# A chunked delta rule with two MoE layers: triangular inverses by 16-row blocks, joined by TensorE

## The chip, the cores and the metric

One core of a Trainium2 chip runs the whole kernel. The metric is device time in microseconds (us), the median of several runs; lower is better. TensorE (PE) multiplies matrices, VectorE (DVE), ScalarE (ACT) and GpSimd (POOL) work elementwise, and SyncE (SP) issues every DMA of this kernel. Each engine takes its own instructions strictly in the order in which they were emitted.

## The reference

```python
def _attn_ref(q, k, v, beta):                 # batch 4, 8 heads, 768 steps, head dim 48
    k_n = k / (norm(k) + 1e-06)
    for t in range(S):
        y[:, :, t] = einsum('bhd,bhde->bhe', q[:, :, t], state)
        v_old = einsum('bhde,bhd->bhe', state, k_n[:, :, t])
        state = state + beta_t * einsum('bhd,bhe->bhde', k_n[:, :, t], v_t - v_old)

x = y, heads side by side                     # (3072, 384)
h = maximum(x @ w_in, 0); x = (h * h) @ w_out                      # d_ff 2048
out = (sigmoid(x @ w_gate) * (x @ w_val)) @ w_out                  # d_ff 1536
```

All of it is float32. The weights arrive as 64-bit floats, and the kernel turns them into pairs of 32-bit parts.

## The kernel before, in words

The sequence is cut into 12 chunks of 64 steps. Two chunks (st 0 and 1) make a **pass** g, so there are 6 passes. In a pass the delta rule is solved for all 32 heads of the batch at once: the products of keys (`am`, token `a`) give a unit triangular 64-by-64 matrix per head and chunk, its inverse is built in `t64`, and with it the chunk's update (`t`), its output (`y`) and the next state (`s`) are matrix products. The pass's output `x` (512 tokens) then goes through the first MoE layer in 16 blocks of 128 hidden features: `h,n` (n is 16 g + block), the squared ReLU on ACT, `g,n` (the low part, on DVE) and `o,n`. The second MoE layer follows after the last pass.

The inverse has two levels. The two 32-by-32 diagonal blocks of each matrix are inverted by substitution on DVE: `ti` transposes `am` into `xi` and clears `tt`, `r,g,i` does three rows j of the substitution (tokens `r,g,0` to `r,g,10`, rows 31 to 1; each row is a multiply at L385 and a subtract at L392, and rows below 22 take two of each), `to` transposes the result back into `t64` and `t1` makes the transposed copy `t1`. TensorE then makes the block beside them from two products, `n` (L414) and `w` (L429), with ACT evicting each.

During passes 0 and 1 the weights of the first MoE layer are also converted, one block f of 16 at a time: `f` loads 768 KB, `hi` (ACT), `b` and `b2` (DVE, two instructions each), `lo` (POOL), `ch` (ACT), `cl` (POOL) and `sl` (a DMA that stores the low part in DRAM). `li,n` and `lw,n` fetch such low parts back; `h,n` and `o,n` cannot run before their block f = n is converted.

The order of everything up to the last blocks of pass 5 is a list written out by hand, `ORDER`. Its tokens are run one after another, and each token emits its instructions on whatever engines it uses. So the list fixes the order within every engine's queue, SP's too, and nothing reorders it afterwards. `xlo`, the low part of `x`, has two buffers in turn.

Of the kernel before, what the change touches and what calls it, by code (L numbers as in the profile page):

```python
# [31 lines left out]
z,0,0 s,0,0 hi,3 f,4 b,2 b2,2 a,1,1 ks,0,1 lo,2 ch,2 cl,2 sl,2 a,1,0 ti,1 x,0,0 ti,1,1 li,1 b,3 t,0,1 hi,4 y,0,1
ti,1,3 b2,3 li,0 s,0,1 z,0,1 x,0,1 f,5 lo,3 ch,3 cl,3 sl,3 r,1,0 r,1,1 f,6 lw,0 v,1,0 kc,1,1 kc,1,0 k2,1,0 q,1,1
hi,5 b,4 h,0 li,2 b2,4 lw,1 g,0 h,1 li,3 lo,4 f,7 b,5 ch,4 cl,4 r,1,2 b2,5 sl,4 q,1,0 lw,2 r,1,3 hi,6 g,1 h,2
li,4 lo,5 f,8 b,6 ch,5 cl,5 r,1,4 b2,6 hi,7 b,7 sl,5 kt,2,1 o,0 lo,6 f,9 ch,6 lw,3 cl,6 sl,6 g,2 h,3 li,5 b2,7
kn,2,0 o,1 r,1,5 r,1,6 hi,8 lw,4 kn,2,1 g,3 h,4 li,6 r,1,7 lo,7 f,10 ch,7 cl,7 hi,9 kt,2,0 sl,7 sq,2,1 r,1,8 o,2
b,8 sq,2,0 lw,5 sv,1,0 b2,8 lo,8 f,11 ch,8 cl,8 r,1,9 hi,10 g,4 h,5 li,7 sl,8 sm,2,0 p,1,0 b,9 r,1,10 b2,9 lo,9
ch,9 cl,9 o,3 lw,6 sl,9 g,5 h,6 li,8 to,1 b,10 hi,11 b2,10 o,4 v,1,1 p,1,1 lw,7 t1,1 lo,10 f,12 ch,10 cl,10 g,6
h,7 li,9 sv,1,1 n,1,0 b,11 b2,11 sl,10 lo,11 f,13 hi,12 ch,11 cl,11 sm,2,1 o,5 n,1,1 ks,1,0 lw,8 sl,11 g,7 h,8
li,10 w,1,0 b,12 b2,12 hi,13 no,2 b,13 o,6 w,1,1 lo,12 ch,12 b2,13 lw,9 cl,12 t,1,0 lo,13 f,14 ch,13 sl,12 cl,13  # L40
a,2,0 g,8 h,9 li,11 sl,13 a,2,1 o,7 lw,10 hi,14 ti,2 g,9 h,10 li,12 y,1,0 ti,2,1 b,14 ti,2,3 z,1,0 b2,14 o,8
s,1,0 lw,11 r,2,0 lo,14 f,15 ch,14 cl,14 sl,14 g,10 h,11 li,13 r,2,1 k2,1,1 hi,15 o,9 lw,12 ks,1,1 x,1,0 b,15
b2,15 r,2,2 g,11 h,12 li,14 t,1,1 y,1,1 z,1,1 lo,15 ch,15 cl,15 r,2,3 o,10 lw,13 sl,15 r,2,4 g,12 h,13 li,15
o,11 lw,14 r,2,5 g,13 h,14 li,16 r,2,6 o,12 lw,15 x,1,1 r,2,7 g,14 h,15 li,17 r,2,8 o,13 kc,2,0 lw,16 w2,0,0
g,15 h,16 li,18 s,1,1 r,2,9 q,2,0 o,14 kn,3,0 lw,17 r,2,10 w2,0,1 g,16 h,17 li,19 kn,3,1 o,15 kc,2,1 v,2,0 lw,18
sq,3,0 w2,0,2 po,0 k2,2,0 sq,3,1 g,17 h,18 li,20 w2,0,3 to,2 o,16 lw,19 kt,3,1 sm,3,0 kt,3,0 w2,0,4 t1,2 p,2,0
g,18 h,19 li,21 sm,3,1 w2,0,5 sv,2,0 n,2,0 w2,1,0 o,17 lw,20 no,3 g,19 h,20 li,22 q,2,1 w2,1,1 o,18 lw,21 ks,2,0
g,20 h,21 li,23 n,2,1 w,2,0 w2,1,2 o,19 w2,1,3 lw,22 a,3,0 g,21 h,22 li,24 w2,1,4 a,3,1 v,2,1 o,20 w,2,1 lw,23
w2,1,5 ti,3 t,2,0 w2,2,0 g,22 h,23 li,25 k2,2,1 sv,2,1 y,2,0 o,21 z,2,0 lw,24 ti,3,1 ti,3,3 w2,2,1 g,23 h,24
li,26 s,2,0 r,3,0 o,22 lw,25 w2,2,2 p,2,1 r,3,1 g,24 h,25 li,27 ks,2,1 w2,2,3 o,23 lw,26 r,3,2 w2,2,4 g,25 h,26  # L50
li,28 w2,2,5 t,2,1 r,3,3 o,24 x,2,0 w2,3,0 lw,27 g,26 h,27 li,29 y,2,1 r,3,4 o,25 lw,28 w2,3,1 g,27 h,28 li,30
# [28 lines left out]
"""  # L80

@with_exitstack
def kernel(
# [18 lines left out]
    nc = tc.nc  # L102
# [3 lines left out]
    work = ctx.enter_context(tc.tile_pool(name="work", bufs=2))  # L106
# [61 lines left out]
    at = ExitStack()  # L168
# [44 lines left out]
    for i in range(NF2 * 3 // 2):  # L213
        cs = slice(i * 2 * DM, (i + 1) * 2 * DM)
# [15 lines left out]
    def att_ps():  # L230
        return ps_a.tile([128, 512], F32, tag="att", name="att")
# [135 lines left out]
    def turn_in(g, q=None):  # L370
# [203 lines left out]
    po = [None] * KD  # L574
# [35 lines left out]
    def keep_warm(n):  # L610
# [232 lines left out]
```

## Time and profile before

| | |
|---|---|
| median of 3 runs | 1154.88 us (1154.48 to 1156.91) |
| the profiled execution | 1156.59 us, its span 1154.9 us |
| PE busy | 1034.7 us, 90% of the span |
| DVE busy | 613.3 us, 53% |
| ACT, POOL busy | 426.6 us, 143.8 us |
| mean granted clock of TensorE | 0.971 of full speed |

The shares are means over a start in which PE is often idle and a long rest in which it is nearly always busy. What a change in the start is worth has to be read from the start alone.

### The profile page before, as it was taken

The numbers are of one execution on the slowest core, as the hardware profiler recorded it, in microseconds if no ns is written. First come the engines' busy times: TensorE is split into PE (matmuls) and PEld (weight loads), VectorE is DVE, ScalarE is ACT, GpSimd is POOL, SyncE is SP. The second block draws the span as 40 slices with busy tenths as digits, with TensorE's granted clock in tenths as the row PEclk, the third lists the DMA queues.
The fourth block names the chain that finished last, engine by engine and source line by source line (L and its number), as shares of the span: only waits on it lengthen the run. The fifth ranks groups of instructions, "written<-read, shape, count | busy, mean of one in ns | idle before, by whom it ended". The sixth has DMA issues, their size and how long they took to land.

```text
span 1154.9 us, 24743 instructions
## 1 busy us (share of the span) xinstructions
PE 1034.7 (90%) x10608; PEld 874.2 (76%) x10608; DVE 613.3 (53%) x1250; ACT 426.6 (37%) x680; POOL 143.8 (12%) x106
## 2 busy tenths in 40 slices
PE   2184757899999999899999999999999999999997
PEld 2173545677787787688888888888888888888886
DVE  5968999986797689389443244322222222222222
ACT  2043435445456355344745564321222222222211
POOL 2122435302002001101110010100100001001000
PEclk9997787899999999899999999999999999999999
DMA  9325933577469447746744554101010010100101
GB/s 254 91 84 145 293 106 128 168 206 208 132 186 283 153 150 225 181 137 192 210 126 160 185 171 137 42 15 41 1 56 1 1 55 1 55 1 1 28 1 28
DMA packets 85214, 133.84 MB, mean 116 GB/s; under 512 B 33648, under 2 KB 66032, under 8 KB 85104
## 3 DMA queue, kind: packets, MB, share of 16 engines
q1 hardware_dynamic: 85104, 132.26, 38.8%
q8 instruction: 83, 1.36, 0.5%
q14 instruction: 27, 0.22, 0.1%
HBM read 104.69 MB, written 22.81 MB: 110 GB/s over the span
## 4 chain that ended last, share of the span: by engine, by line
PE 78%; DVE 11%; DMA 4%; SPq 2%; issue 2%; ACT 2%; POOL 1%; DVEq 0%; ACTq 0%; POOLq 0%
PE gv L716 26%; PE o L586 14%; PE h L549 14%; PE o L746 13%; DVE tt L392 3%; DVE tmp L385 2%; PE att L343 2%; PE att L472 1%; PE att L494 1%; DMA il<-w1d 1%; DVE wt L141 1%; DMA w1d<-wl 1%; DMA kc<-in_kq_dram 1%; PE att L460 1%; PE att L496 1%
## 5 line engine op out<-in xcount | busy, mean ns | idle before, releaser
L724 DVE TENSOR_TENSOR p<-sg,gv 128x512 f32<-128x512 f32 x72 | 49.5, 687 | 284.1 <-PE gv L716 284.1
L716 PE MATMUL gv<-xhi,w2l 128*128 128x512 f32 x432 | 123.3, 394 | 0.0
L716 PE MATMUL gv<-xhi,w2h 128*128 128x512 f32 x432 | 123.3, 394 | 0.0
L716 PE MATMUL gv<-xlo,w2h 128*128 128x512 f32 x432 | 123.2, 393 | 0.0
L562 ACT ACTIVATE gg<-h 128x512 f32<-128x512 f32 x96 | 57.2, 596 | 169.5 <-PE h L549 148.4
L586 PE MATMUL o<-gh,il 128*128 128x512 f32 x288 | 114.8, 399 | 0.0
L722 ACT ACTIVATE sg<-gv 128x512 f32<-128x512 f32 x72 | 43.0, 598 | 182.2 <-PE gv L716 182.2
L726 ACT CAST ph<-p 128x512 fp32r<-128x512 f32 x72 | 44.7, 620 | 159.0 <-DVE p L724 159.0
L586 PE MATMUL o<-gl,w1h 128*128 128x512 f32 x216 | 87.0, 403 | 13.0 <-DVE gl L571 13.0
L549 PE MATMUL h<-xhi,il 128*128 128x512 f32 x288 | 84.9, 404 | 14.1 <-DMA il<-w1d 14.1
L746 PE MATMUL o<-w2h,pl 128*128 128x384 f32 x288 | 97.4, 338 | 0.0
L746 PE MATMUL o<-w2h,ph 128*128 128x384 f32 x288 | 97.2, 338 | 0.0
L746 PE MATMUL o<-w2l,ph 128*128 128x384 f32 x288 | 97.1, 337 | 0.0
L716 PEld LDWEIGHTS gv<-xlo,w2h 128*128 128x128 f32 x432 | 81.3, 188 | 18.9
L716 PEld LDWEIGHTS gv<-xhi,w2l 128*128 128x128 f32 x432 | 81.1, 188 | 18.8
L571 DVE TENSOR_TENSOR gl<-gg,gh 128x512 fp32r<-128x512 f32 x96 | 71.7, 748 | 42.8 <-ACT gg L565 42.7
L392 DVE TENSOR_TENSOR tt<-tt,tmp 128x21 f32<-128x21 f32 (+37 forms) x312 | 90.2, 322 | 2.1
L586 PE MATMUL o<-gh,w1h 128*128 128x512 f32 x216 | 90.3, 418 | 0.0
L716 PEld LDWEIGHTS gv<-xhi,w2h 128*128 128x128 f32 x432 | 80.3, 188 | 12.8
L385 DVE TENSOR_TENSOR tmp<-xi,tt 128x21 f32<-128x21 f32 (+37 forms) x312 | 83.4, 300 | 1.3
L549 PEld LDWEIGHTS h<-xhi,il 128*128 128x128 f32 x288 | 55.8, 195 | 27.9 <-DMA il<-w1d 15.7
L728 DVE TENSOR_TENSOR pl<-p,ph 128x512 fp32r<-128x512 f32 x72 | 49.9, 692 | 49.4 <-ACT ph L726 49.4
(111 smaller groups left out, 1768.5 us busy)
## 6 DMA issues: line engine op xcount, KB each, us to landing
il<-w1d SPq DMA_DIRECT2D x192, 192.0 KB, 3.6
raw<-in_w_dram SPq DMA_DIRECT2D x25, 768.0 KB, 6.0
w1s<-in_w_dram SPq DMA_DIRECT2D x9, 768.0 KB, 6.0
w2d<-y SPq DMA_DIRECT2D x18, 384.0 KB, 3.9
t<-w2d SPq DMA_DIRECT2D x12, 576.0 KB, 3.8
w1d<-wl SPq DMA_DIRECT2D x16, 384.0 KB, 2.8
kn<-in_kn_dram SPq DMA_DIRECT2D x12, 384.0 KB, 4.8
v<-in_vn_dram SPq DMA_DIRECT2D x12, 384.0 KB, 5.2
```

Of the source, the lines that this page charges most:

```text
L385: nc.vector.tensor_tensor(out=tv[i], in0=xi[:, 0:j, j].unsqueeze(2).to_broadcast([128, j, n]), in1=tt[:, j, lo:hi].unsqueeze(1).to_broadca ...
L392: nc.vector.tensor_tensor(out=tt[:, 0:j, lo:hi], in0=tt[:, 0:j, lo:hi], in1=tv[i], op=ALU.subtract)
L549: nc.tensor.matmul(out=ps[:, cs], lhsT=w[:, kc * 128:kc * 128 + 128], rhs=x[:, kc, cs], start=(i == 0 and kc == 0), stop=(i == 2 and kc == ...
L562: nc.scalar.activation(out=gg, in_=ps, func=ACTF.Relu)
L571: nc.vector.tensor_tensor(out=gl, in0=gg, in1=gh.bitcast(F32), op=ALU.subtract)
L586: nc.tensor.matmul(out=po[m], lhsT=w[:, cs], rhs=x, start=(f == 0 and i == 0), stop=(f == NF1 - 1 and i == 2),)
L716: nc.tensor.matmul(out=ps, lhsT=w[:, kc * 128:kc * 128 + 128], rhs=x[:, kc, :], start=(i == 0 and kc == 0), stop=(i == 2 and kc == KD - 1),)
L722: nc.scalar.activation(out=sg, in_=pss[0], func=ACTF.Sigmoid)
L724: nc.vector.tensor_tensor(out=p, in0=sg, in1=pss[1], op=ALU.mult)
L726: nc.scalar.copy(out=ph, in_=p)
L728: nc.vector.tensor_tensor(out=pl, in0=p, in1=ph.bitcast(F32), op=ALU.subtract)
L746: nc.tensor.matmul(out=po2[m], lhsT=x[:, cs], rhs=w, start=(f == 0 and i == 0), stop=(f == NF2 - 1 and i == 2),)
```

## The change

In passes 0 and 1 the substitution covers only the 16-by-16 diagonal blocks: 15 rows instead of 31, both blocks of a 32-by-32 block in one instruction (`row16`). The 32-by-32 inverse is then joined from its parts by TensorE: `ja` (a product of `am` and `t64` on top of minus the identity, which a 128-column matmul with `ib` and `cb` puts there first), `jb` (a product with `t1`) and `jc` (the same for the transposed copy), with evictions on ACT. `cj` makes the constants on POOL, in a tile that takes a buffer of `xlo` before its use. Passes 2 to 5 keep the 32-row substitution. The rest of the change is a new `ORDER` list.

```diff
+BLOCK = (16, 16, 32, 32, 32, 32)
 ORDER = """
-kn,0,1 v,0,0 kt,0,0 sq,0,1 sm,0,1 q,0,0 kn,0,0 sq,0,0 v,0,1 f,1 be kt,0,1 kc,0,0 sm,0,0 no,0 cs hi,1 f,0 kn,1,0
+v,0,0 kn,0,1 kn,0,0 kt,0,0 sq,0,1 be kt,0,1 sm,0,1 sq,0,0 f,1 kc,0,0 q,0,0 v,0,1 sm,0,0 no,0 hi,1 f,0 cs q,0,1
...
+    join_t = work.tile([128, KD * GT], F32, tag="xlo", name="join")
+    nf = join_t[:, 0:1024].rearrange("p (u c) -> p u c", u=32)
+    cb = join_t[:, 1024:1280].bitcast(BF16).rearrange("p (u c) -> p u c", u=32)
+    ib = join_t[:, 1280:1344].bitcast(BF16)
...
+    def join_constants():
+        for t, v in ((ib, 1.0), (cb, -1.0), (nf[:, :, 0:16], 1.0)):
+            nc.gpsimd.memset(t, v)
+        def diagonal(t, pattern, base):
+            nc.gpsimd.affine_select(
+                out=t, in_=t, pattern=pattern, base=base, channel_multiplier=-1, compare_op=ALU.is_equal, fill=0.0
+            )
+        diagonal(ib, [[1, 128]], 0)
+        for q in range(4):
+            diagonal(cb[quad(q)], [[0, 32], [1, 16]], 16)
+            diagonal(nf[quad(q), :, 0:16], [[0, 32], [1, 16]], 0)
+    def both(t, at, *dims):
+        return bass.AP(t.tensor, t.offset + at, [list(t.ap[0]), [16 * 33, 2], *dims])
+    def row16(j):
+        n = 16 - j
+        tv = tmp[1][:, 0:2 * j * n].rearrange("p (b c i) -> p b c i", b=2, i=n)
+        nc.vector.tensor_tensor(
+            out=tv, in0=both(xi, j, [32, j], [0, n]), in1=both(tt, 33 * j, [0, j], [1, n]), op=ALU.mult
+        )
+        t = both(tt, j, [32, j], [1, n])
+        nc.vector.tensor_tensor(out=t, in0=t, in1=tv, op=ALU.subtract)
-    def rows(i):
-        for j in range(31 - 3 * i, max(0, 28 - 3 * i), -1):
-            row(j)
+    def rows(g, i):
+        b = BLOCK[g]
+        for j in range(b - 1 - 3 * i, max(0, b - 4 - 3 * i), -1):
+            (row16 if b == 16 else row)(j)
     def turn_1(g):
         nc.vector.transpose(out=t1.rearrange("p u c -> p c u"), in_=tt)
+        if BLOCK[g] == 32:
+            for q in (0, 2):
+                nc.scalar.copy(out=t64[quad(q), :, 0:32], in_=t64[quad(q), :, 32:64])
+    def join_a(g, i):
+        if i == 0:
+            join_ps[g] = att_ps()
+            nc.tensor.matmul(out=join_ps[g], lhsT=ib, rhs=cb.rearrange("p u c -> p (u c)"), start=True, stop=False)
+        psv = join_ps[g].rearrange("p (u c) -> p u c", u=32)
+        for u in range(16 * i, 16 * i + 16):
+            for q in range(4):
+                c = 32 * (q % 2)
+                nc.tensor.matmul(out=psv[32 * q:32 * q + 16, u, :], lhsT=am[quad(q), u, c:c + 16],
+                                 rhs=t64[quad(q), u, 48:64], start=False, stop=u == 31)
+        if i == 1:
+            nc.scalar.mul(out=nf[:, :, 16:32], in_=psv, mul=-1.0)
+    def join_b(g, i):
...
+                nc.tensor.matmul(out=psv[quad(q), u, :], lhsT=t1[quad(q), u, :], rhs=nf[quad(q), u, 16:32], ...)
+        if i == 1:
+            nc.scalar.copy(out=t64[:, :, 48:64], in_=psv)
+            for q in (0, 2):
+                nc.scalar.copy(out=t64[quad(q), :, 0:32], in_=t64[quad(q), :, 32:64])
+    def join_c(g):
...
+                nc.tensor.matmul(out=psv[quad(q), u, :], lhsT=nf[quad(q), u, :], rhs=t1[quad(q), u, 0:16], ...)
+        for q in (0, 2):
+            nc.scalar.copy(out=t1[quad(q), :, 0:16], in_=psv[quad(q)])
```

What the new list moves is seen in the engines' queues. A matmul counts once here, and the trace has two PE instructions for each float32 one. First SP's queue at the start of the program, before and then changed (`w1s` and `raw` are blocks of weights, `k_114` is the tile `k2`):

```order
L267 DMA kn<-in_kn_dram 128x768
L272 DMA v<-in_vn_dram 128x768
L256 DMA kt<-in_kq_dram 48x1024 x2
L262 DMA q<-in_kq_dram 48x1024 x2
L267 DMA kn<-in_kn_dram 128x768
L272 DMA v<-in_vn_dram 128x768
L126 DMA w1s_137<-in_w_dram 128x1536
L621 DMA beta_t<-in_beta_dram 128x192
L256 DMA kt<-in_kq_dram 48x1024 x2
```

```order
L280 DMA v<-in_vn_dram 128x768
L275 DMA kn<-in_kn_dram 128x768 x2
L264 DMA kt<-in_kq_dram 48x1024 x2
L707 DMA beta_t<-in_beta_dram 128x192
L264 DMA kt<-in_kq_dram 48x1024 x2
L127 DMA w1s_137<-in_w_dram 128x1536
```

The second `kn` load stood behind four loads of other tensors; it is now the third transfer. Next PE's queue in pass 0, between the scores `p` (L343, now L351) and the update `t` (L460, now L546), before and then changed (`t_107` is `t64`, and `xi` holds `t1`):

```order
L343 MATMUL att<-q,kc 64x64 x64
L414 MATMUL att<-t_107,am 32x32 x64
L429 MATMUL att<-n,xi 32x32 x64
L460 MATMUL att<-v,t_107 64x48 x32
L494 MATMUL att<-pm,u_112 64x64 x32
```

```order
L351 MATMUL att<-q,kc 64x64 x64
L451 MATMUL att<-join 128x512
L458 MATMUL att<-t_107,am 16x16 x128
L473 MATMUL att<-join,xi 32x16 x128
L488 MATMUL att<-xi,join 32x16 x64
L500 MATMUL att<-t_107,am 32x32 x64
L515 MATMUL att<-n,xi 32x32 x64
L546 MATMUL att<-v,t_107 64x48 x32
```

The join's 321 matmuls stand ahead of `n` and `w`. Last DVE's queue in pass 1, around the second half of pass 0's `x` (`xlo<-xr`), before and then changed:

```order
L481 TENSOR_TENSOR state<-state,att 128x8x48 x2
L115 TENSOR_TENSOR xlo<-xr,xhi 128x3x256
L385 TENSOR_TENSOR tmp_111<-xi,tt 128x31
L392 TENSOR_TENSOR tt<-tt,tmp_111 128x31
L385 TENSOR_TENSOR tmp_111<-xi,tt 128x60
L392 TENSOR_TENSOR tt<-tt,tmp_111 128x30x2
```

```order
L407 TENSOR_TENSOR tmp_111<-xi,tt 128x110
L411 TENSOR_TENSOR tt<-tt,tmp_111 128x2x11x5
L407 TENSOR_TENSOR tmp_111<-xi,tt 128x120
L411 TENSOR_TENSOR tt<-tt,tmp_111 128x2x10x6
L116 TENSOR_TENSOR xlo<-xr,xhi 128x3x256
L567 TENSOR_TENSOR state<-state,att 128x8x48 x2
L138 TENSOR_SCALAR y<-wt 128x768
```

The first six rows of pass 1's substitution now stand ahead of that `xlo`, and the two state additions behind it.

## Rows read from the trace of the kernel before

**Rows 1.** Busy us by stretch (instructions), engines PE, PEld, DVE, ACT, POOL; then clock, DMA, GB/s.
```profile
0.00:100.00 100.00, 41.75 (x1152) 38.76 (x1152) 70.75 (x169) 26.14 (x39) 21.86 (x27) 0.97 0.49 131
100.00:230.00 130.00, 88.82 (x1297) 70.62 (x1298) 125.08 (x214) 55.16 (x85) 51.89 (x28) 0.80 0.59 181
230.00:260.00 30.00, 28.72 (x179) 23.11 (x178) 26.76 (x104) 13.71 (x22) 2.29 (x1) 0.99 0.70 200
260.00:1155.00 895.00, 875.41 (x7984) 741.71 (x7982) 390.68 (x764) 331.57 (x536) 67.72 (x50) 0.99 0.34 102
```
**Rows 2.** Waits of DVE and PE, 100 to 230: total us, times, longest.
```profile
DVE xlo L115 <- ACT xhi L114: 5.4, 2, 4.5
PE o L586 <- DVE gl L571: 13.0, 3, 8.0
PE h L549 <- DMA il<-w1d: 12.8, 1, 12.8
```
**Rows 3.** Timeline of the start: start us, us, engine, line, operation.
```profile
7.73 1.98 PE L332 MATMUL att<-kt 48*64 48x64 f32 x62 [0.60 <-DMA kt<-in_kq_dram]
10.60 0.84 ACT L289 ACTIVATE kn<-kn 128x768 f32<-128x768 f32 x1 [5.62 <-DMA kn<-in_kn_dram]
22.32 3.81 DVE L376 STREAM_TRANSPOSE xi<-am 32x1024 f32<-32x1024 f32 x2
```
**Rows 4.** Timeline of DVE in pass 0's substitution.
```profile
28.83 0.19 DVE L385 TENSOR_TENSOR tmp<-xi,tt 128x31 f32<-128x31 f32 x1
29.81 0.25 DVE L385 TENSOR_TENSOR tmp<-xi,tt 128x87 f32<-128x87 f32 x1
30.10 0.25 DVE L392 TENSOR_TENSOR tt<-tt,tmp 128x87 f32<-128x87 f32 x1
34.18 1.29 DVE L349 TENSOR_TENSOR pm<-att,mask 128x512 f32<-128x512 f32 x2 [0.38 <-PE att L343]
46.70 0.55 DVE L137 TENSOR_SCALAR y<-wt 128x768 uint32<-128x768 uint32 x1
47.28 0.96 DVE L141 SCALAR_TENSOR_TENSOR wt<-wt,y 128x768 uint32<-128x768 uint32 x1
54.39 0.95 DVE L294 TENSOR_REDUCE s<-kn 128x16 f32<-128x768 f32 x1
57.26 2.18 DVE L401 STREAM_TRANSPOSE t<-tt 128x1024 f32<-128x1024 f32 x1
```
**Rows 5.** Busy us of L385 alone, then L392, in passes 0 and 1.
```profile
28.83:57.25 28.42, 12.10 (x52) 1.00 0.39 93
101.00:163.10 62.10, 19.67 (x52) 0.75 0.73 221
...
28.83:57.25 28.42, 13.54 (x52) 1.00 0.39 93
101.00:163.10 62.10, 18.32 (x52) 0.75 0.73 221
```
**Rows 6.** Timeline of ACT and PE: a pair of small evictions, and small matmuls.
```profile
61.61 1.20 ACT L420 ACTIVATE n<-att 32x512 f32<-32x512 f32 x2
65.02 1.91 PE L429 MATMUL att<-n,xi 32*32 32x32 f32 x62 [0.18 <-ACT n L420]
72.23 3.44 PE L472 MATMUL att<-u,k 64*64 64x48 f32 x60 [0.52 <-ACT yt L499]
183.34 1.20 PE L429 MATMUL att<-n,xi 32*32 32x32 f32 x64
```
**Rows 7.** Timeline of POOL: start-up work, and a weight step beside a DVE multiply.
```profile
1.02 0.53 POOL L357 TENSOR_SCALAR_AFFINE_SELECT mask<-mask 64x64 f32<-64x64 f32 x2
4.63 0.30 POOL L364 MEMSET state<- 128x256 f32 x1
100.91 1.86 POOL L206 TENSOR_TENSOR wl<-wt,w1h 128x768 fp32r<-128x768 f32 x1 [4.31 <-ACT w1h L202]
101.01 1.82 DVE L385 TENSOR_TENSOR tmp<-xi,tt 128x31 f32<-128x31 f32 x1
```

More of the change, by code (lines that the diff above doesn't have):

```diff
@@ L32 @@
[L32 to L51, printed above, removed]
@@ new lines @@
+t1,3 g,33 h,34 li,36 po,1 sv,3,0 p,3,0 w2,5,1 o,32 lw,35 kt,4,1 sm,4,0 kt,4,0 sm,4,1 g,34 h,35 li,37 kc,3,1
+w2,5,2 n,3,0 o,33 ks,3,0 w2,5,3 lw,36 no,4 g,35 h,36 li,38 v,3,1 w2,5,4 n,3,1 w,3,0 o,34 k2,3,0 w2,6,0 lw,37
+w2,5,5 g,36 h,37 li,39 w,3,1 o,35 q,3,1 lw,38 a,4,0 t,3,0 w2,6,1 g,37 h,38 li,40 a,4,1 k2,3,1 o,36 sv,3,1 y,3,0
+w2,6,2 lw,39 ti,4 g,38 h,39 li,41 w2,6,3 s,3,0 z,3,0 ti,4,1 o,37 lw,40 w2,6,4 ti,4,3 p,3,1 g,39 h,40 li,42 r,4,0
+w2,7,0 w2,6,5 o,38 ks,3,1 lw,41 g,40 h,41 li,43 r,4,1 w2,7,1 o,39 lw,42 t,3,1 r,4,2 g,41 h,42 li,44 w2,7,2
@@ new lines @@
+kc,5,1 o,58 lw,61 r,5,5 w2,12,4 g,60 h,61 li,63 w2,13,0 w2,12,5 r,5,6 o,59 q,5,0 lw,62 x,4,1 g,61 h,62 li,64
+r,5,7 w2,13,1 o,60 lw,63 s,4,1 g,62 h,63 li,65 w2,13,2 r,5,8 o,61 w2,13,3 lw,64 r,5,9 g,63 h,64 li,66 p,5,0
+w2,13,4 r,5,10 o,62 lw,65 v,5,0 w2,13,5 g,64 h,65 li,67 to,5 o,63 lw,66 po,3 sv,5,0 t1,5 g,65 h,66 li,68 n,5,0
+ks,5,0 o,64 q,5,1 w2,14,0 lw,67 g,66 h,67 li,69 n,5,1 v,5,1 w,5,0 o,65 k2,5,1 lw,68 t,5,0 w2,14,1 g,67 h,68
+li,70 k2,5,0 w,5,1 o,66 w2,14,2 lw,69 g,68 h,69 li,71 w2,14,3 y,5,0 o,67 sv,5,1 lw,70 w2,14,4 w2,15,0 g,69 h,70
@@ new lines @@
+li,72 s,5,0 w2,14,5 o,68 lw,71 p,5,1 g,70 h,71 li,73 ks,5,1 w2,15,1 o,69 z,5,0 lw,72 w2,15,2 g,71 h,72 li,74
+w2,15,3 o,70 t,5,1 lw,73 w2,15,4 g,72 h,73 li,75 x,5,0 w2,16,0 o,71 w2,15,5 lw,74 y,5,1 g,73 h,74 li,76 z,5,1
+w2,16,1 o,72 lw,75 g,74 h,75 li,77 w2,16,2 o,73 w2,16,3 lw,76 g,75 h,76 li,78 w2,16,4 o,74 w2,17,0 lw,77 w2,16,5
+g,76 h,77 li,79 o,75 lw,78 w2,17,1 g,77 h,78 li,80 o,76 x,5,1 w2,17,2 lw,79 g,78 h,79 li,81 w2,17,3 o,77 lw,80
+w2,17,4 g,79 h,80 li,82 w2,17,5 o,78 lw,81 g,80 h,81 li,83 o,79 lw,82 po,4 g,81
@@ L404, in turn_1 @@
         nc.vector.transpose(out=t1.rearrange("p u c -> p c u"), in_=tt)
+        if BLOCK[g] == 32:
+            for q in (0, 2):
+                nc.scalar.copy(out=t64[quad(q), :, 0:32], in_=t64[quad(q), :, 32:64])
+    join_ps = {}
+    def join_a(g, i):
+        if i == 0:
+            join_ps[g] = att_ps()
+            nc.tensor.matmul(
+                out=join_ps[g], lhsT=ib, rhs=cb.rearrange("p u c -> p (u c)"), start=True, stop=False
+            )
+        psv = join_ps[g].rearrange("p (u c) -> p u c", u=32)
+        for u in range(16 * i, 16 * i + 16):
+            for q in range(4):
+                c = 32 * (q % 2)
+                nc.tensor.matmul(
+                    out=psv[32 * q:32 * q + 16, u, :], lhsT=am[quad(q), u, c:c + 16], rhs=t64[quad(q), u, 48:64],
+                    start=False, stop=u == 31,
+                )
+        if i == 1:
+            nc.scalar.mul(out=nf[:, :, 16:32], in_=psv, mul=-1.0)
+            del join_ps[g]
+    def join_b(g, i):
+        if i == 0:
+            join_ps[g] = att_ps()
+        psv = join_ps[g].rearrange("p (u c) -> p u c", u=32)
+        for u in range(16 * i, 16 * i + 16):
+            for q in range(4):
+                nc.tensor.matmul(
+                    out=psv[quad(q), u, :], lhsT=t1[quad(q), u, :], rhs=nf[quad(q), u, 16:32], start=True, stop=True
+                )
+        if i == 1:
+            nc.scalar.copy(out=t64[:, :, 48:64], in_=psv)
+            for q in (0, 2):
+                nc.scalar.copy(out=t64[quad(q), :, 0:32], in_=t64[quad(q), :, 32:64])
+            del join_ps[g]
+    def join_c(g):
+        ps = att_ps()
+        psv = ps.rearrange("p (u c) -> p u c", u=32)
+        for u in range(32):
+            for q in (0, 2):
+                nc.tensor.matmul(
+                    out=psv[quad(q), u, :], lhsT=nf[quad(q), u, :], rhs=t1[quad(q), u, 0:16], start=True, stop=True
+                )
         for q in (0, 2):
-            nc.scalar.copy(out=t64[quad(q), :, 0:32], in_=t64[quad(q), :, 32:64])
+            nc.scalar.copy(out=t1[quad(q), :, 0:16], in_=psv[quad(q)])
     def n_piece(g, st):
@@ L621 @@
         k2=load_k2, be=lambda: nc.sync.dma_start(out=beta_t, in_=beta), cs=constants, sq=squares, sm=sums, no=norms,
-        a=scores_a, sv=scale_v, p=scores_p, ti=turn_in, r=lambda g, i: rows(i), to=turn_out, t1=turn_1,
+        a=scores_a, sv=scale_v, p=scores_p, ti=turn_in, r=rows, cj=join_constants, ja=join_a, jb=join_b, jc=join_c, to=turn_out, t1=turn_1,
         n=n_piece, w=w_piece, ks=ks_piece, t=t_piece, s=s_piece, y=y_piece, x=x_split, d=keep_warm,
```

67 lines of the change are left out of this document (36 added, 31 removed).

## The prediction

> **What bounds the kernel now.** I read the busy times by stretch first, then the waits, then the timeline of the start. The stretches [rows 1] show three states. To 100 us PE works 42 of 100 us. From 100 to 230 PE works 89 of 130 us while DVE works 125: DVE is the bound. From 230 on PE is: 28.7 of 30 us, then 875 of 895. What is won before 230 therefore reaches the end undiminished, as long as the PE work behind it stays the same, and what is done for DVE after 230 is worth nothing.
>
> In the DVE-bound stage the waits of PE say how DVE paces it [rows 2]: 13.0 us for `gl`, which stands in DVE's queue behind rows of the substitution, and 12.8 us for one low part from DRAM, the end of the conversion of a weight block whose DVE steps stand in the same queue. DVE itself waited only 5.4 us, nearly all of it once, 4.5 us for the first pass's `x`. Ahead of the stage the path is a chain: loads, norms, three transposes, pass 0's substitution, the two products `n` and `w`, the update, `y`, its transfer, `x`.
>
> **The change part by part.**
>
> *Loads and norms.* The second `kn` load was the seventh transfer issued, and its square started at 10.60; transfers three and four, the first `kt` pair, had landed by 7.73 [rows 3]. It is now the third, so I put its square at 7.7. From that square to the end of the last transpose (22.32 + 3.81 = 26.13) the chain took 15.5 us and is the same now: the substitution can start at 23.2. Before it started at 28.83 [rows 4], since a conversion step and a mask multiply stood ahead of it; in the new list those come later. The end of the loads that this rests on could lie 2 us to either side.
>
> *The constants (`cj`).* They are nine selects and three memsets on POOL behind the start-up work that ends at 4.9, ahead of the memset of `tt` that the first row needs. A select of 64 columns takes 0.27 us [rows 7]. Most of the new ones have 512 columns: at least 0.27 us each (2.4 us for nine), at most eight times that (2.2 us, some 18 us for eight and a small one). They end between 8 and 24 us. I take the middle, where they are hidden by the 23.2 above; the upper end costs some 2 us.
>
> *Pass 0's substitution.* Before, it ran from 28.83 to 57.26, 28.4 us. In it lie two conversion steps (0.55 + 0.96 each), a mask pair with its wait (1.7) and a reduction (0.95), 5.7 us together [rows 4]: the 31 rows cost 22.7 us, of which about 1.5 is one held instruction. Now there are 15 rows of two instructions with 30 to 128 elements, 91 on the mean. One of 87 elements is followed by the next after 0.29 us (29.81 to 30.10), so 30 of them cost 8.6 us. The new list puts three conversion steps and two mask pairs between, 7.1 us. The transpose `to` then starts at 23.2 + 8.6 + 7.1 = 38.9 and ends at 41.1; before it ended at 59.4.
>
> *The join in pass 0.* This is the added cost, and it stands on the path: `ja`, an eviction, `jb`, `jc`, and only then `n`, since all are in PE's queue ahead of it and feed each other. That is 320 small matmuls, 640 PE instructions in the trace. The other eviction of `jb` and the copies of `t64`, which only moved, run on ACT beside `jc`; the copies of `jc` stand where those of `t64` stood. The critical eviction costs about 0.7 us with its hand-over (the pair in [rows 6] takes 1.20). For the matmuls no row has 16 columns. L429, with 32, takes 31 ns each at this place (1.91 us for 62) and 19 ns later (1.20 us for 64). Half of the latter, 9.5 ns, is the lower bound if columns alone counted, and 57 ns (L472, 3.44 us for 60) the upper. I take 22 ns, near L429's two rows but for half the columns: 14.1 us.
>
> The Trainium skill says otherwise here: TensorE: Matmul & The Clock Gate, section "Wait — 56ns, not 53.3ns?", has starts never closer than about 25 ns however few the columns. The row at 183.34 contradicts it with 19 ns. By the page's figure the join would cost 16 us and the whole gain be 2 us smaller.
>
> From the end of `to` to the end of `w` the kernel before took 66.9 − 59.4 = 7.5 us [rows 4, 6]. Now: 41.1 + 14.1 + 0.7 + 7.5 = 63.4, which is 3.5 us earlier. So most of what DVE saves in pass 0 goes to PE; with 19 ns it is 5.4 us earlier, with 31 ns it is 2.3 later. Behind `w` the chain to the first `h` is unchanged, and DVE, free 18 us earlier, has nothing to do in it that would be late.
>
> *Pass 1.* Here the rows stand in the stage in which DVE is the bound, so they count in full. Before, all 31 came behind pass 0's last `xlo`. Without what holds them they cost as in pass 0 (22.7 less the 1.5), 21.2 us. Now six of the 15 stand ahead of that `xlo`, where DVE waited 4.5 us [rows 2], and their 3.4 us fit. Nine remain: 18 instructions of 97 elements, 0.29 us each, 5.3 us. Two state additions of together 1.0 us move behind the `xlo`. The stage loses 21.2 − 5.3 − 1.0 = 15 us (14.9).
>
> Can the other queues follow? The stage has 130 − 15 = 115 us. PE had 88.8 and gets 640 × 19 ns = 12 us more, 101. ACT has 55 and gets some 3; POOL 52; the DMA share rises from 0.59 to 0.67. None is at its limit, but PE's slack falls from 41 to 14 us, and its order is fixed: it now waits for three more hand-overs (`to`, two evictions) with `h` and `o` queued behind. The list puts `h` or `o` between the parts, so I add nothing, and keep the case that it doesn't suffice as a rival.
>
> *Passes 2 to 5* keep their instructions. The new list changes their order, but PE had only some 20 us of idle time in the last 895, the output's tail included; I take no change, with 5 us to either side.
>
> *Sum.* 3.5 + 14.9 = 18.4 us. The profiled execution took 1156.59 (span 1154.9); the median of the runs is 1154.88, so I take the difference off that: **1136 us**.
>
> **The rivals.**
>
> *A second bound takes over in pass 1.* PE's slack of 14 us is spread over waits it can't choose, and the conversion chain (DVE, POOL, ACT, POOL, a DMA out, a DMA in, all of them in order) has its own pace. For it: the wait of 12.8 us for a low part. Against it: DVE waited for nothing but `x`, and the chain's other engines are half idle. If a third of the 14.9 remains, the gain is 3.5 + 5 = 8.5: 1146 us.
>
> *The held DVE instructions go too.* In pass 1 the two lines were busy 38.0 us against 25.6 in pass 0 for the same work [rows 5], 12.4 us more. A multiply of 31 elements took 1.82 us beside a POOL step of 1.86 [rows 7], where 0.19 is its own time. If the hold belongs to the rows, five sixths of it (86 of 104 instructions are gone or lie earlier) go with them, 10 us more; with 19 ns in pass 0 that is 5.4 + 14.9 + 10 = 30: 1125 us. Against it: POOL's steps stay as many, and would hold whatever DVE runs instead.
> The Trainium skill takes this second side: GPSIMD Engine Reference, section "8. Key points", has GpSimd sharing its SBUF interfaces with VectorE and contending with instructions that have two SBUF inputs, as most of the conversion's have. The row at 101.01 agrees that the hold is POOL's. By it the hold moves rather than goes, and 1136 stands.
>
> *Slower: small matmuls at the slow pace.* The join's matmuls come in the same few corners of the array, as L472's do, which took 57 ns each. At that price pass 0's join costs 36.5 us, `w` ends at 41.1 + 36.5 + 0.7 + 7.5 = 85.8, 18.9 us late, and pass 1 gives back 14.9 at most: 1159 us. The point from which it decides: 49.3 + 0.64 p = 66.9 + 14.9 gives p = 51 ns. Against it: L429, the nearest in shape, has 31.
>
> *It doesn't do what it says.* That the 15 rows cost as much as 31 would need twice the time per element for the two-block pattern; then 8.6 us go in pass 0 and 5.3 in pass 1, and 4.5 of the gain are left: 1150 us. I count it with the first rival.
>
> **How the numbers follow.** Forecast 0.53, own range 1128 to 1143 (19 and 31 ns, and the 2 us of the loads). The second bound 0.22, the hold 0.14, the slow matmuls 0.08, and 0.03 for a later order that eats the gain to nothing. Faster by over 0.2% (2.3 us, about what a measurement can tell) is 0.53 + 0.22 + 0.14 = 0.89; within it 0.03; slower 0.08. For 8 in 10 the range takes in the forecast and most of the two rivals beside it: 1121 to 1149.
>
> **What would show it right or wrong.** Right: the first row at 23 us and `to` near 39; the 640 join instructions at 19 to 25 ns; the first `h` 1 to 6 us earlier than before; DVE above 90% busy from there until PE saturates near 212 instead of 230; nothing else changed behind. Wrong: `ja` at 31 ns or more; the first `h` later than before; PE waiting at the join's parts in pass 1 for more than 5 us in all; DVE idle for long in that stage, which would name a second bound; POOL's constants ending later than 23 us.

## The result and the profile after

The changed kernel takes 1143.61 us (median of 4 runs, 1142.21 to 1144.12) against 1155.89 for the kernel before on the same chip (1154.48 to 1157.17): a ratio of 0.9892, 95% interval 0.9875 to 0.9909. In a second set of runs it was 0.9905 (0.9882 to 0.9928). The forecast was 1136, its range 1121 to 1149. So the time lies in the range, with 5.6 us less gain in the trace (12.8 us of span, where 18.4 were forecast). It lies just outside the narrower 1128 to 1143 that the forecast's own story was given, on the side of the first rival's 1146.

The page's first part and the busy times by stretch, cut at 232 instead of 230 us, answer to [rows 1]; the columns are the same.

```profile
span 1142.1 us, 27177 instructions
## 1 busy us (share of the span) xinstructions
PE 1054.6 (92%) x11890; PEld 893.0 (78%) x11890; DVE 580.6 (51%) x1102; ACT 430.7 (38%) x688; POOL 152.8 (13%) x118
```

```profile
0.00:100.00 100.00, 53.81 (x1794) 49.68 (x1794) 60.29 (x106) 29.17 (x44) 31.95 (x40) 1.00 0.52 139
100.00:232.00 132.00, 106.94 (x1984) 85.67 (x1985) 111.83 (x170) 62.32 (x95) 52.99 (x28) 0.87 0.63 192
232.00:260.00 28.00, 28.00 (x319) 23.21 (x319) 26.05 (x82) 15.99 (x26) 2.90 (x2) 1.00 0.91 238
260.00:1143.00 883.00, 865.84 (x7808) 734.42 (x7801) 382.43 (x746) 323.22 (x524) 64.97 (x48) 0.99 0.34 100
```

PE has 12 us more work ahead of 100 us than before, and the first `h` starts no earlier. Four marks of the timeline say where the gain is: the end of `to` in pass 0, the end of `w`, the start of the first `h`, and the end of `y` for the second chunk of pass 1, behind which PE is saturated. I call the stretch between the last two the stage of pass 1.

| us | `to` | `w` | first `h` | `y`(1,1) | stage | rest of the span |
|---|---|---|---|---|---|---|
| before | 59.44 | 66.93 | 100.16 | 229.12 | 129.0 | 925.8 |
| forecast | 41.1 | 63.4 | 96.7 | 210.7 | 114.1 | as before |
| after | 43.07 | 66.43 | 99.95 | 216.37 | 116.4 | 925.7 |

(The forecast's first `h` and `y` are its 3.5 and 14.9 us taken off.) The start gained 0.2 us, the stage 12.5, the rest 0.1. All later runs are read by these marks. How far one profile can be trusted is seen in a second one of the same kernel, from the last set of runs below: `w` ends at 67.71 there and the first `h` starts at 100.73, 1.3 and 0.8 us later, while the stage, 116.6, is the same.

**The start.** PE's timeline where `ja` (L458), `jb` (L473) and `jc` (L488) run, ahead of `n` (L500) and `w` (L515): start, us, engine, line, operation, count, and in brackets the idle time before it with its releaser.

```profile
43.13 2.01 PE L458 MATMUL att<-t,am 32*16 32x16 f32 x219 [6.06 <-DVE t L437]
47.47 0.49 PE L458 MATMUL att<-t,am 32*16 32x16 f32 x37 [2.33 <-issue]
48.67 1.46 PE L473 MATMUL att<-join,xi 32*32 32x16 f32 x91 [0.71 <-ACT join L463]
51.40 1.90 PE L473 MATMUL att<-join,xi 32*32 32x16 f32 x128 [1.27 <-issue]
54.86 0.67 PE L473 MATMUL att<-join,xi 32*32 32x16 f32 x35 [1.56 <-issue]
...
55.37 2.60 PE L488 MATMUL att<-xi,join 32*32 32x16 f32 x90
58.31 1.03 PE L488 MATMUL att<-xi,join 32*32 32x16 f32 x31 [0.34 <-issue]
```

PE is fast inside a run of `ja` or `jb`: 219 in 2.01 us are 9 ns each, 128 in 1.90 are 15. (`jc`, which goes to two of the array's corners in turn and not to four, takes 29 inside its run.) But then PE stands idle with no releaser but "issue": first after 219, then after each further 128 (37 + 91, 128, and so on). The clock is not what slows it: it stood at 1.00 in the first run and behind it (43.00 to 45.20 and on to 47.40 us, columns as in [rows 1]).

```profile
43.00:45.20 2.20, 2.01 (x219) 1.92 (x220) 2.20 (x3) 0.00 (x0) 0.00 (x0) 1.00 0.03 7
45.20:47.40 2.20, 0.00 (x0) 0.00 (x0) 2.17 (x4) 0.00 (x0) 1.07 (x1) 1.00 0.00 0
```

The DMA queue of instructions shows what comes at that pace. From 43 to 60 us, in 40 slices of 0.425 us:

```profile
GB/s 0 0 0 0 39 0 0 0 0 0 0 0 0 39 0 0 0 0 0 0 0 0 39 0 0 0 0 0 0 0 39 0 0 0 0 0 0 0 39 0
DMA packets 5, 0.08 MB, mean 5 GB/s; under 512 B 0, under 2 KB 0, under 8 KB 0
## 3 DMA queue, kind: packets, MB, share of 16 engines
q8 instruction: 5, 0.08, 1.9%
```

A packet of 16 KB comes every 8 or 9 slices, 3.4 to 3.8 us. The page's count of that queue for the whole program (packets, MB, share), before and then after:

```profile
q8 instruction: 83, 1.36, 0.5%
```

```profile
q8 instruction: 93, 1.52, 0.6%
```

That is ten more for 2564 more PE instructions (1282 matmuls and as many weight loads), so one brings 256, that is 128 matmuls. The kernels of the experiments keep to it: 10608 matmul instructions came with 83 packets, 11249 with 88, 11570 with 90, 11890 with 93 and 12146 with 95. The trace also has the time of each packet:

| pause (us) | first | second | third | fourth |
|---|---|---|---|---|
| packet, start to end | 44.86 to 46.07 | 48.84 to 49.95 | 52.46 to 53.35 | 55.90 to 56.79 |
| PE goes on at | 47.47 | 51.40 | 54.86 | 58.31 |

PE goes on 1.4 to 1.5 us after a packet has ended, and the next packet starts 1.0 to 1.4 us after PE went on. So I read the pauses as PE waiting for its instructions: some 3.5 us per 128, 27 ns each. The large matmuls of `h` start some 230 ns apart (three in 0.68 us at 125 us), so that 128 of them outlast a packet's 3.5 us by far.

**The stage of pass 1.** Engines over its whole length, before and then after (columns as in [rows 1]):

```profile
100.16:229.12 128.96, 87.94 (x1295) 69.95 (x1295) 124.21 (x213) 54.38 (x82) 51.56 (x28) 0.80 0.60 182
```

```profile
99.95:216.37 116.42, 95.51 (x1936) 76.92 (x1936) 97.00 (x127) 55.89 (x85) 49.25 (x26) 0.85 0.66 200
```

DVE lost 27.2 us of work, far more than the 14.9 forecast, but the stage became only 12.5 us shorter. DVE was 96% busy and is now 83% busy; it is no longer alone what holds the stage. (TensorE's granted clock rose from 0.80 to 0.85 in it; what that gave back was not measured.) The waits of PE in it, from 99.95 to 216.37, which answer to [rows 2] (total us, times, longest), and two of DVE's:

```profile
PE h L635 <- ACT xhi L115: 6.1, 1, 6.1
PE h L635 <- DMA il<-w1d: 5.4, 1, 5.4
PE att L473 <- ACT join L463: 4.7, 1, 4.7
...
PE att L488 <- issue: 2.4, 1, 2.4
...
PE o L672 <- DVE gl L657: 1.6, 1, 1.6
```

```profile
DVE gl L657 <- ACT gg L651: 8.8, 2, 7.6
DVE s L302 <- ACT kn L297: 3.3, 1, 3.3
```

The two old waits, for `gl` and for the low part, fell from 13.0 and 12.8 to 1.6 and 5.4. New ones are the join's eviction, 4.7 (2.8 in the second profile), and DVE's waits for ACT. The chain of work that ended last, followed back from 150 us (start, us, what), names two places:

```profile
101.80 8.17 DMA kc<-in_kq_dram
109.99 5.90 SPq L613
...
139.57 0.91 ACT wt L133
140.48 0.49 ACT join L463
```

First, pass 1's loads of `kc`, which `li` (L613, a fetch of low parts) and then the weights' DMAs stand behind in SP's queue. Second, the eviction of `ja`, whose matmuls had ended at 134.3: in ACT's queue it stands behind `hi` of block 9 (L133), which waits for POOL's part of the block before.

### The profile page after: what moved, and what is told of

The parts are those of the page before. It is cut to its first block, busy times and chain, and to the rows that moved or that the text cites. A ratio compares the mean times of both kernels' runs of the same rounds, so it can differ in the third digit from the quotient of the medians.

```text
span 1142.1 us, 27177 instructions
## 1 busy us (share of the span) xinstructions
PE 1054.6 (92%) x11890; PEld 893.0 (78%) x11890; DVE 580.6 (51%) x1102; ACT 430.7 (38%) x688; POOL 152.8 (13%) x118
## 4 chain that ended last, share of the span: by engine, by line
PE 84%; DVE 6%; DMA 3%; SPq 2%; issue 2%; ACT 1%; POOL 1%; ACTq 0%; DVEq 0%; POOLq 0%
PE gv L802 26%; PE h L635 16%; PE o L672 16%; PE o L832 13%; PE att L351 2%; PE att L558 2%; PE att L340 1%; PE att L546 1%; PE att L500 1%; PE att L580 1%; PE att L515 1%; PE att L528 1%; DMA il<-w1d 1%; PE att L582 1%; DMA w1d<-wl 1%
## 5 line engine op out<-in xcount | busy, mean ns | idle before, releaser
L802 PEld LDWEIGHTS gv<-xhi,w2h 128*128 128x128 f32 x432 | 80.3, 188 | 12.8
L116 POOL TENSOR_TENSOR xlo<-x2r,xhi 128x512 fp32r<-128x512 f32 x18 | 24.6, 1368 | 398.8 <-ACT xhi L115 398.8
L635 PE MATMUL h<-xhi,w1h 128*128 128x512 f32 x216 | 67.6, 423 | 6.1 <-ACT xhi L115 6.1
```

Source lines behind the costliest of these rows:

```text
L116: eng.tensor_tensor(out=dst_lo, in0=src, in1=dst_hi.bitcast(F32), op=ALU.subtract)
L635: nc.tensor.matmul(out=ps[:, cs], lhsT=w[:, kc * 128:kc * 128 + 128], rhs=x[:, kc, cs], start=(i == 0 and kc == 0), stop=(i == 2 and kc == ...
L802: nc.tensor.matmul(out=ps, lhsT=w[:, kc * 128:kc * 128 + 128], rhs=x[:, kc, :], start=(i == 0 and kc == 0), stop=(i == 2 and kc == KD - 1),)
```

## The experiments

I had two questions, and a theory and a rival for each. On the start, theory A: the join of pass 0 costs PE at least what it saves DVE, since its matmuls come at the pace of their instructions. Theory B: the join pays there as forecast, and its matmuls cost what the array takes. On the stage, theory C: the loads and the eviction behind `hi,9` hold it. Theory D: DVE's remaining work, or another engine's, does, so moving them gives little. In the last set theory A speaks for A and C together. The texts put down before the runs use the letters A and B anew for the pair that each run decides, and say in brackets which it is.

**The 31 rows back in pass 0.**

```diff
-BLOCK = (16, 16, 32, 32, 32, 32)
+BLOCK = (32, 16, 32, 32, 32, 32)
-... r,0,4 ch,0 cl,0 sq,1,1 to,0 t1,0 ja,0,0 kt,1,1 sq,1,0 kt,1,0 ja,0,1 jb,0,0 b2,1 lo,1 sl,0 jb,0,1 jc,0 n,0,0 ...
+... r,0,4 r,0,5 r,0,6 r,0,7 r,0,8 r,0,9 r,0,10 ch,0 cl,0 sq,1,1 to,0 t1,0 kt,1,1 sq,1,0 kt,1,0 b2,1 lo,1 sl,0 n,0,0 ...
```

> The changed kernel, but pass 0 takes all 31 rows on VectorE again and has no join; the list is otherwise the new one. Theory A (in pass 0 the join of 640 PE instructions, 16 us, costs as much as the 16 rows that it saves): the last transpose ends near 57 instead of 43, but w ends near 65 instead of 66.4, and the time is 1142 us, 1 to 2 below the changed kernel. Theory B (the join in pass 0 carries its share of the gain, as predicted, 3.5 us and more): 1147 us.

Measured: 1143.28 us, ratio 0.9855 (0.9816 to 0.9893). `to` ends at 55.43, 12.4 us later than with the join, and yet `w` ends at 63.65, 2.8 us earlier, and the first `h` starts at 97.72 instead of 99.95. The join of pass 0 is a net loss in the start: A. The ratio itself can't be told from the changed kernel's, but the marks of eight profiles agree. With the changed kernel's pass 0 (two profiles of that kernel, the next run, and `hi,9` below) `w` ends at 65.9 to 67.7 and the first `h` starts at 99.95 to 101.7; with 31 rows there (this run, the list alone, and two of the kernel with all three edits) they are 62.6 to 63.7 and 96.6 to 97.9.

**The 31 rows back in pass 1 alone.**

```diff
-BLOCK = (16, 16, 32, 32, 32, 32)
+BLOCK = (16, 32, 32, 32, 32, 32)
-... r,1,4 to,1 b,7 cl,6 ... hi,9 t1,1 ja,1,0 o,2 sv,1,0 b,8 lw,5 ja,1,1 p,1,1 ... jb,1,0 ... jb,1,1 sl,8 sm,2,0 jc,1 ...
+... r,1,4 b,7 r,1,5 cl,6 ... r,1,7 h,4 li,6 sl,7 hi,9 o,2 sv,1,0 b,8 lw,5 p,1,1 r,1,8 ... to,1 sl,8 sm,2,0 t1,1 ...
```

> The changed kernel, but pass 1 takes all 31 rows on VectorE again, spread over the list as far as its blocks 5 to 9, and has no join. Theory A (the whole gain is VectorE's time in the stage of pass 1): 1154 to 1156 us, as before the change. Theory B (the new list brings half of it): 1148 us or less.

Measured: 1154.57 us, ratio 0.9964 (0.9946 to 0.9981). First `h` at 100.71, stage 126.7. Nearly the whole gain is gone, as theory A of this run said, so it is pass 1's join that makes it.

**The new list with no join at all.**

```diff
-BLOCK = (16, 16, 32, 32, 32, 32)
+BLOCK = (32, 32, 32, 32, 32, 32)
```

(and the two edits of the list above, without `cj` and its tile.)

> The new list with 31 rows in both passes and no join and no constants for it. Theory A: the earlier loads of pass 0 show (first row at 23 instead of 29), w ends 2 us earlier than before the change, and the time is 1152 to 1154 us, some 2 below the kernel before. Theory B (the list is what counts): 1146 us or less.

Measured: 1151.27 us, ratio 0.9936 (0.9904 to 0.9969). This lies 0.7 below the 1152 to 1154 of its theory A, and far above the 1146 of B. `to` ends at 54.34, `w` at 62.56, first `h` 96.61, stage 127.2. The list alone brings the first `h` 3.6 us forward and takes 1.7 off the stage. Joining in pass 1 then takes 10.6 more off the stage (127.2 to 116.7 in the first experiment); joining in pass 0 gives 2.2 back (97.72 to 99.95).

**`jb` of pass 0 issued twice.**

```diff
-            for q in range(4):
+            for q in [0, 1, 2, 3] * (2 if g == 0 else 1):
```

> The changed kernel with the 128 matmuls of jb in pass 0 done twice over (the second set writes the same values). Theory A (in pass 0 a long run of small matmuls is paced by the arrival of PE's instructions, about 3.4 us per 128 matmul instructions, 27 ns each, however fast the array is): 256 more cost 6.9 us, with gaps of issue between runs of 128, and w ends near 73.3 instead of 66.4. Theory B (the array's own pace of 10 to 15 ns, as within the runs of jb): 2.5 to 3.9 us, w ends at 69 to 70.3.

Measured in a single execution: 1150.34 us. `w` ends at 73.79, 7.36 us later for 256 more matmul instructions, 28.7 ns each. A expected 73.3, B 70.3 at most; the unchanged start ended between 65.9 and 67.7. The timeline of `jb` (here L471):

```profile
48.57 1.46 PE L471 MATMUL att<-join,xi 32*32 32x16 f32 x91 [0.70 <-ACT join L461]
51.02 1.90 PE L471 MATMUL att<-join,xi 32*32 32x16 f32 x128 [1.00 <-issue]
54.76 1.90 PE L471 MATMUL att<-join,xi 32*32 32x16 f32 x128 [1.83 <-issue]
58.48 1.90 PE L471 MATMUL att<-join,xi 32*32 32x16 f32 x128 [1.82 <-issue]
```

Every 128 start 3.7 us after the last, 1.90 of it work.

**Pass 0's join with half the instructions.** It reads the upper 16 bits of its operands as bf16, so each product is one PE instruction instead of two, and of lower precision.

```diff
+    def one(g, x):
+        return x.bitcast(BF16)[:, 1::2] if g == 0 else x
-    lhsT=am[quad(q), u, c:c + 16], rhs=t64[quad(q), u, 48:64],
+    lhsT=one(g, am[quad(q), u, c:c + 16]), rhs=one(g, t64[quad(q), u, 48:64]),
```

(and likewise in `jb` and `jc`.)

> The changed kernel with pass 0's join in one PE pass: it reads the upper 16 bits of each float32 operand as bfloat16, so ja, jb and jc of pass 0 lose precision and have 320 PE matmul instructions instead of 640. Theory A (instruction delivery): 320 fewer at 25 to 27 ns, 8 us, w ends near 58.5. Theory B (the join is mostly hand-overs between engines): only half of PE's busy time in the join goes, 5 us, w ends near 61.5.

Measured in a single execution: 1126.51 us; `w` at 57.79 (A 58.5, B 61.5), first `h` at 90.37. 320 fewer instructions took 8.64 us off, 27.0 ns each. (The rest of the 17 us is not the join's: the stage took 113.9 us and the rest of the span 920.2, some 5 less than in every other kernel here, and one execution can't say why.) The timeline (`n` is L501 here):

```profile
43.09 1.17 PE L459 MATMUL att<-t,am 32*16 32x16 bf16 x128 [6.05 <-DVE t L435]
45.01 0.88 PE L474 MATMUL att<-join,xi 32*32 32x16 bf16 x91 [0.75 <-ACT join L464]
47.26 0.43 PE L474 MATMUL att<-join,xi 32*32 32x16 bf16 x37 [1.37 <-issue]
47.52 1.02 PE L489 MATMUL att<-xi,join 32*32 32x16 bf16 x64
48.41 0.95 PE L501 MATMUL att<-t,am 32*32 32x32 f32 x27
51.26 2.72 PE L501 MATMUL att<-t,am 32*32 32x32 f32 x95 [1.89 <-issue]
```

The first pause comes after 128 + 91 = 219 matmul instructions again, the next after 37 + 64 + 27 = 128, though these are other matmuls of another type, and the second pause lies in the middle of `n`. What counts is the instructions, not the work in them. That settles A against B. That the packets bring them is read from their number and their times: in this run and the one before, too, all eight pauses end 1.2 to 1.6 us after the end of a packet. No run varied the packets themselves.

**The loads of pass 1 earlier.**

```diff
-... jb,0,1 jc,0 n,0,0 ... t,0,0 no,1 ... s,0,1 sl,3 kc,1,1 v,1,0 kc,1,0 q,1,0 h,0 ...
+... jb,0,1 jc,0 kc,1,1 q,1,0 n,0,0 ... t,0,0 v,1,0 no,1 ... s,0,1 sl,3 kc,1,0 h,0 ...
```

> The changed kernel with three loads of pass 1 (one kc, q and v, 1.15 MB) taken out of the queue ahead of the fetch that h,2 waits for and put between 43 and 70 us, where the DMA engines stand nearly idle. Theory C (the second bound of the stage is the DMA queue between 100 and 130 us, with a wait of 5.4 us of PE and SP held for 5.9 us): that wait goes and the time falls by 3 to 5 us, to 1139. Theory D (the wait is repaid by the next one, VectorE or ScalarE): 1142 to 1144.

Measured: 1146.05 us, ratio 0.9886 (0.9846 to 0.9926), no gain: neither C's 1139 nor D's 1142 to 1144. The stage fell to 114.0, 2.4 us less, with its waits for low parts at 3.8 instead of 5.4. But it began 2.2 us later and ended only 0.2 earlier, at 216.19. So this run alone does not show that time is won there; the run with all three edits does, for the loads and `hi,9` together.

`w` ended 1.9 us later, at 68.32. `to` was 0.9 late already, and the first row of the substitution 0.8 (24.01), before the moved loads were issued; the rest came in the join, where the pauses before `jb`'s third part and `jc`'s second grew from 1.56 to 2.11 and from 0.34 to 0.61, and `w` got one of 0.38. That the loads delay the instructions can't be read from this. The second profile of the changed kernel, without the edit, has pauses of 1.83, 0.89 and 0.52. And the place in the list is not the time of issue: SP issued the loads of `kc` and `q` at 35.7 and 36.6 us and that of `v` at 70.3, not between 43 and 70 as was expected. From 44 to 60 us only the packets of instructions moved (43 to 60 us, as above):

```profile
GB/s 202 87 0 0 0 0 39 0 0 0 0 0 0 0 39 0 0 0 0 0 0 0 0 39 0 0 0 0 0 0 0 0 0 39 0 0 0 0 0 0
```

Why the start was late in this run stays open.

**`hi,9` behind `ja`'s eviction.**

```diff
-... h,4 li,6 sl,7 hi,9 t1,1 ja,1,0 o,2 sv,1,0 b,8 lw,5 ja,1,1 p,1,1 ...
+... h,4 li,6 sl,7 t1,1 ja,1,0 o,2 sv,1,0 b,8 lw,5 ja,1,1 hi,9 p,1,1 ...
```

> The changed kernel with one token moved: the ScalarE step hi,9, which waits for a buffer of the weight conversion and stands in ScalarE's queue ahead of the eviction of ja in pass 1, is put behind that eviction. Theory A (PE's wait of 4.7 us for the eviction is part of what holds the stage): the wait goes, the time falls by 2 to 4 us against the changed kernel, to 1140 on the same chip. Theory B (VectorE and the conversion hold the stage anyway): no change within 1 us.

Measured: 1142.17 us, ratio 0.9858 (0.9821 to 0.9894). The wait for the eviction fell from 4.7 (2.8 in the second profile) to 1.8 us, DVE's wait for a square behind those matmuls from 7.6 to 1.1, and the stage from 116.4 to 111.8; it ended at 213.5, 2.9 earlier though it began later. The start was 1.7 us later in that profile, so the total can't be told from the changed kernel's; the stage can.

**All three: 31 rows in pass 0, earlier loads, `hi,9` later.** Here the loads of `kc` and `q` are issued at 30 to 31 us and that of `v` at 66, not between 45 and 70.

```diff
-BLOCK = (16, 16, 32, 32, 32, 32)
+BLOCK = (32, 16, 32, 32, 32, 32)
+... to,0 t1,0 kc,1,1 q,1,0 kt,1,1 sq,1,0 ... t,0,0 v,1,0 no,1 ... ja,1,1 hi,9 p,1,1 ...
```

> Three edits on the changed kernel: 31 rows on VectorE and no join in pass 0, three loads of pass 1 issued between 45 and 70 us, and hi,9 behind the eviction of ja in pass 1. If each acts by itself (first h 2.2 us earlier, the stage 2.5 us shorter, and up to 3 for hi,9): 5 to 8 us below the changed kernel, 1136 to 1139. If the stage is held by VectorE once the waits are gone: 3 us below, 1141.

Measured: 1134.2 us, ratio 0.9778 (0.9737 to 0.9818), more than either expectation. First `h` at 97.92, stage 110.9. The first experiment has the same pass 0 without the two moves, its first `h` at 97.72 and a stage of 116.7. So the two moves take 5.8 us off the stage: C. `hi,9` alone had taken 4.6; the loads' own share was not separated.

**The same again, beside the changed kernel and one more.** The third kernel has the changed kernel's joins, both reading only the upper 16 bits as above, with the loads (`kc` and `q` behind `w` in its list) and `hi,9` moved.

> The changed kernel once more, so that the two others have it on their own chip. Every theory: ratio to the kernel before 0.987 to 0.991.

> The 31 rows back in the first pass, with the earlier loads and hi,9 behind ja,1,1, once more. Theory A (the join of pass 0 costs more than it saves, and the stretch of pass 1 was held by its loads and by the eviction queued behind hi,9): ratio 0.975 to 0.982, about 1% below the changed kernel on the same chip. Rival (the three edits only trade among themselves): within 0.4% of the changed kernel.

> The changed kernel with the joins of both passes reading only the upper 16 bits of their operands (half the matmul instructions, lower precision), the loads earlier and hi,9 behind ja,1,1. Theory A (the joins are paced by the delivery of their instructions): first h at about 90 us, stretch of pass 1 107 to 110 us, in all 1118 to 1122 us. Rival (pass 1 is held by VectorE's work, whatever the joins cost): stretch 112 to 114, in all 1124 to 1127 us.

Measured on one chip, 5 rounds: the changed kernel 1146.53 us, 0.9905 (0.9882 to 0.9928). The three edits together 1135.01, 0.9812 (0.9783 to 0.9841): the intervals don't touch, so at full precision this is faster than the kernel before and, by 11.5 us, than the changed one. The one-pass joins 1128.76, 0.9756 (0.9729 to 0.9782): first `h` at 90.41 and stage 109.9 as theory A said, but my total for it (1118 to 1122) was missed, as was the rival's (1124 to 1127). The two marks and the unchanged 925 us behind them make 1125.4, its span; the total had been summed too low.

The stages of these two last kernels are equal, with twice the join instructions in the first:

```profile
96.96:206.96 110.00, 94.98 (x1936) 76.03 (x1936) 97.35 (x127) 55.93 (x85) 49.02 (x26) 0.88 0.65 201
```

So in pass 1, where large matmuls lie between the join's parts, the delivery of instructions costs the stage nothing that shows, as far as two kernels can tell that differ in pass 0 too. DVE's work is what it was after the change (97.0 us); the 6.4 us came out of its waiting.

## Why the prediction was right, and where it was off

The direction and the main mechanism held: nearly all of the gain comes from pass 1's rows, in the stage that DVE held, and the 925 us behind came out as before. By its steps:

- **Loads and norms:** right, the exact hit by luck. The first row started at 23.17, forecast 23.2. The square stood at 6.83 instead of 7.7, and the chain from it to the last transpose took 16.2 us instead of 15.5; the two errors cancel.
- **`cj`:** right. The nine selects took 6.92 us and ended at 13.0, between the bounds of 8 and 24, and nothing waited.
- **Pass 0's substitution:** `to` started at 40.90 instead of 38.9. The rows themselves cost what was said (30 times 0.29 is 8.7, not 8.6). The 2 us are two DVE instructions held beside POOL steps, which the sum had left out though it had one such in its 22.7:

```profile
29.95 2.46 DVE L142 SCALAR_TENSOR_TENSOR wt<-wt,y 128x768 uint32<-128x768 uint32 x1
...
33.53 0.96 DVE L407 TENSOR_TENSOR tmp<-xi,tt 128x126 f32<-128x126 f32 x1
```

```profile
29.40 2.19 POOL L158 TENSOR_TENSOR wt<-wt,w1s 128x768 f32<-128x768 f32 x1 [9.81 <-DVE w1s L151]
32.53 1.81 POOL L207 TENSOR_TENSOR wl<-wt,w1h 128x768 fp32r<-128x768 f32 x1 [0.94 <-ACT w1h L203]
```

The first takes 0.96 at 25.18, the like of the second 0.29 at 35.50: 1.5 and 0.7 us of hold.

- **The join in pass 0:** 16.0 us from `ja` to `jc` (43.13 to 59.14), forecast 14.8. The size was nearly met, the reasoning not: 22 ns was taken as a price by columns between L429's 19 and 31, but `ja` and `jb` run at 9 to 16, `jc` at 29, and the instructions come at 27. The Trainium skill's figure that the prediction set aside (TensorE: Matmul & The Clock Gate, section "Wait — 56ns, not 53.3ns?", starts at least 25 ns apart) gives the better estimate, 16 us, but not for its reason: 219 matmuls started 9 ns apart here, in a stretch with a granted clock of 1.00, which is 2.4 GHz.
- **What pass 0's join is worth:** the step that failed. Of 3.5 us forecast 0.5 came by the end of `w`: 2.0 went to the held steps and 1.1 to what lies between `to` and the end of `w`. And the 3.5 itself mixed two parts. The list alone, with the earlier start, brings `w` to 62.56; the join then costs 3.9 (2.8 in the run with pass 1's join). I had compared the join with the old list's `to`, not with 31 rows begun as early.
- **Pass 1:** 12.5 us of 14.9, and two errors lie in this one number. That it came out near is luck: two of the rivals, one for 1125 us and one for 1146, came true together and nearly cancelled. DVE lost 27.2 us of work in the stage, since the rival "the held instructions go too" was right: the rows' busy time in pass 1 fell from 38.0 [rows 5] to 12.7 us. Of it, the multiplies and then the subtracts after (stretch, its length, busy, clock, DMA, GB/s):

```profile
78.00:130.00 52.00, 5.83 (x15) 0.93 0.80 231
```

```profile
78.00:130.00 52.00, 6.89 (x15) 0.93 0.80 231
```

  In pass 0 the same rows took 8.3, so the hold on them fell from 12.4 to 4.4. The Trainium skill's rule (GPSIMD Engine Reference, section "8. Key points", shared interfaces) agrees with the rows above on what holds: both held steps have two inputs in SBUF. But the prediction's conclusion that the hold only moves is contradicted: of the conversion's four DVE steps two have two inputs (not most, as it said), and the twelve of each of these in the stage went from 25.7 to 27.8 us, so 2.1 of 8.0 us moved to them. The eleven `gl`, with two inputs as well, fell from 11.4 to 8.1. The rival "a second bound takes over" was right too: DVE's idle time in the stage went from 4.8 to 19.4 us. With the loads and `hi,9` moved the stage became 6.4 us shorter, out of that idle time. What holds the 110 us that are left was not settled.
- **What would show it wrong** was named and came: PE waited 7.1 us at the join's parts in pass 1 (4.7 and 2.4; the bound was 5), and DVE was 83% busy instead of over 90%.
- **The slow matmuls** (57 ns) did not come: the 640 of pass 0 took 16.0 us with their hand-over, 25 ns each, and 27 to 29 where more of them followed one another.

## What to carry to other kernels

Price work moved to TensorE by the number of its instructions where many small ones stand alone on the path. In a stage where PE had idle time and large matmuls lay between, their number cost nothing that showed. Price each part of a change against the kernel with all its other parts, not against the old one. When the bound engine gets 27 us lighter, the stage follows only as far as the other queues' order lets it; look up what is next in those queues before adding the gain up.

## What the runs showed that was not expected

- A long run of small matmuls is not paced by the array: 219 run at 9 ns each, and then PE pauses at every 128, in the middle of any step, to a mean of 27 to 29 ns. 320 fewer of 640 instructions took 8.6 us off the start, 256 more added 7.4. Every pause in the three traces shown ended 1.2 to 1.6 us after a packet of instructions had.
- Two DVE steps with two inputs in SBUF, beside a POOL step, were held until the POOL step's end, or nearly (2.46 us instead of 0.96, ending at 32.4 where POOL's took until 31.6; 0.96 instead of 0.29, ending at 34.5 where POOL's ended at 34.3). Of the hold that rows had suffered in pass 1, two thirds (8.0 of 12.4 us) went with the rows, and 2.1 of that came back on the conversion's steps.
